# Storing a group's output: one transfer instead of four, in a fused attention and expert kernel on one core

## The chip, the core and the metric

The kernel runs on one core of one Trainium2 chip. The metric is the device time of a run in microseconds, lower is better. A profile is one execution of the program, recorded by the hardware; its times are microseconds from the start of the span, the time from the first to the last recorded instruction.

The engines go by the profile's names: PE (TensorE, matrix products), PEld (its weight loads), DVE (VectorE), ACT (ScalarE), POOL (GpSimd) and SP (SyncE, which only issues transfers). Transfers (DMA) are issued by SP, ACT and POOL and carried out by sixteen DMA engines.

## The reference

Four batches of 12480 tokens of 128 channels pass an attention with 32 inducing points, and then a two-layer net with a leaky activation:

```python
B, N, m, C = (4, 12480, 32, 128)
...
def mab(q, kv):
    s = scale * (q @ kv.transpose(0, 2, 1))
    s = s - s.max(-1, keepdims=True)
    a = np.exp(s)
    a /= a.sum(-1, keepdims=True) + 1e-09
    return a @ kv
h = mab(I, x)
return mab(x, h).astype(np.float32)
...
n_tokens, d_model, d_ff = (49920, 128, 2048)
...
h = x @ w_in
g = np.maximum(h, 0.0) + alpha * np.minimum(h, 0.0)
return (g @ w_out).astype(np.float32)
```

Inputs and output are float32. The output is 49920 x 128, 25.6 MB.

## The kernel before

A batch is cut into six blocks of 2048 tokens and a rest of 192; a block holds four groups of 512 tokens, so that a batch has 25 groups and the whole has 100. Phase A of a batch reads x (loads on POOL's queue, L412, L415, L427, with the change to bfloat16 on the way), transposes it (transfers on SP's queue, L432), takes scores against the inducing points (L553) and sums up the 32 vectors h of the batch. Batch 0's phase A stands by itself at the start; that of each later batch is woven into the groups of the batch before. Phase B works group by group. `b_scores` takes the scores of a block against h (ACT, L656), which go to DRAM (tile e2d, SP, L663); `b_rep` reads them back four times, once for each quarter of the partitions (tile rep, four transfers on SP, L671). `b_den` and `b_turn` do the same for the reciprocals of the softmax's sums (rt, L701; rdT, four transfers, L711).

`fill` makes the hidden layer: 16 small products of hW and rep for a group, each on a quarter of PE's rows (L383 is the line of the helper that records every product), with the positive part taken by ACT (L750) or DVE (L752) into a tile gt. `second` multiplies the gt tiles by W1 into the group's output bank, and after the last one calls `finish`.

`finish` is what the change touches. DVE transposes the bank in 32 x 32 blocks to the tile ot (L818; the pool has two buffers). POOL multiplies it by the reciprocals into the tile ob (L826; three buffers); for the group before the last, POOL does one half and DVE the other; for the last group DVE does all. Then the group is stored to DRAM (L851). Because of the block transpose, partition 32a + i of ob holds column block a (32 columns) of the tokens that belong to i, so the store writes rows of 32 floats, 128 bytes each: 512 rows for each of the four column blocks, 2048 for a group of 512 tokens, and 192 rows a block for the rest of a batch. The stores of most groups go out on POOL's queue; those of the last four groups on SP, ACT and POOL, by the table `queues`, where `to_end` counts the groups that are still to finish (0 is the last).

The order on each engine is fixed: `pin` ties every instruction to the one before it on its engine. What PE does in which order is written out in PLAN, one letter for each product; EVENTS and PAUSES say at which group and fill the loads, transposes, scores, reads and turns are issued. A store stands in POOL's order right behind the multiplication of its group, and the next x load, if there is one, behind the store. The batch changes are at groups 25, 50 and 75: the scores of the new batch's first block can be made only once its h is there (PAUSES, `hw1 bs10` at group 21, `hw2 bs20` at 46, `hw3 bs30` at 71), and its rep is read at the first fill of the new batch.

Of the kernel before, what the change touches and what calls it, by code (L numbers as in the profile page):

```python
# [19 lines left out]
NQ = 4  # L20
# [287 lines left out]
def kernel(  # L308
# [9 lines left out]
    nc = tc.nc  # L318
# [20 lines left out]
    def pin(bi):  # L339
        ins = bi.ins  # L340
        e = ins.engine
        if e in last:
            tc.add_manual_dep(
                ins,
                last[e],
                mybir.DependencyInfo(
                    mybir.DependencyClass.NoSync, mybir.DependencyReason.DATA
                ),
                reason="program order",
            )  # L350
        last[e] = ins.name
        return bi
# [361 lines left out]
    def shape_of(g):  # L714
        return (P, NB, 1) if g < NS * NQ else (PR, JR, 2)
# [68 lines left out]
    def second(i, n, r):  # L784
        st, g = group_of(i)
        pp, nb, _ = shape_of(g)
        t = pp * nb
        rows = slice(0, P) if r is None else slice(32 * r, 32 * r + 32)
        c, gt = live[i][n]
        first = i < LATE and n == 0 and not r  # L790
        if r and n == 0:
            hand_over(left[i])
        ins = mm(
            home[i][:, :t], W1[rows, c, :], gt[rows, :],
            start=first, stop=False, skip_group_check=True,
        )
        if n == KC - 1:
            if r == 3 or r is None:
                if i < LATE:
                    linear(st, g, home[i], 3, False)  # L800
                finish(st, g, home.pop(i))
                live.pop(i)
            else:
                left[i] = ins.ins
# [4 lines left out]
    def finish(st, g, acc):  # L809
        pp, nb, _ = shape_of(g)  # L810
        t = pp * nb
        s, q = divmod(g, NQ)
        rq = st.rden[s][:, :, :, q : q + 1]
        rbc = bass.AP(
            tensor=rq.tensor, offset=rq.offset, ap=[rq.ap[0], rq.ap[1], rq.ap[2], [0, 32]]
        )
        ot = ot_pool.tile([P, GRP], f32, name="ot", tag="ot")
        pin(nc.vector.transpose(out=ot[:, :t], in_=acc[:, :t]))  # L818
        ob = ob_pool.tile([P, GRP], f32, name="ob", tag="ob")
        to_end = B * NG - 1 - ended[0]  # L820
        ended[0] += 1

        def scaled(engine, k0, k1):
            w = t // nb
            part = rbc[:, k0:k1]
            pin(engine.tensor_tensor(  # L826
                out=ob[:, k0 * w : k1 * w].rearrange("p (k m c) -> p k m c", k=k1 - k0, c=32),
                in0=ot[:, k0 * w : k1 * w].rearrange("p (k m c) -> p k m c", k=k1 - k0, c=32),
                in1=part, op=MULT,
            ))  # L830

        if to_end == 0:
            scaled(nc.vector, 0, nb)
        elif to_end == 1:
            scaled(nc.gpsimd, 0, nb // 2)
            scaled(nc.vector, nb // 2, nb)
        else:
            scaled(nc.gpsimd, 0, nb)
        t0 = st.b * N + s * SUP
        if s < NS:  # L840
            dst = out[t0 : t0 + SUP, :].rearrange(
                "(i b q) (a k) -> q a i b k", b=t // 32, q=NQ, k=32)[q]
        else:
            dst = out[t0 : t0 + REM, :].rearrange("(i b) (a k) -> a i b k", b=t // 32, k=32)
        queues = {
            3: (nc.sync,) * 4, 2: (nc.scalar,) * 4,
            1: (nc.sync, nc.scalar, nc.gpsimd, nc.sync),
            0: (nc.scalar, nc.gpsimd, nc.scalar, nc.sync),
        }.get(to_end, (nc.gpsimd,) * 4)
        for a, queue in enumerate(queues):  # L850
            pin(queue.dma_start(  # L851
                out=dst[a],
                in_=ob[32 * a : 32 * a + 32, :t].rearrange("p (b k) -> p b k", k=32),
            ))
        st.rep.pop(g)

# [47 lines left out]
    for q in range(4):  # L904
        sl = slice(32 * q, 32 * q + 32)
        pin(nc.gpsimd.memset(pick[sl, q : q + 1], 1.0))
        for q2 in range(4):
            pin(nc.gpsimd.tensor_copy(
                out=fold[sl, 32 * q2 : 32 * q2 + 32], in_=ident32[sl, sl]
# [63 lines left out]
    n = len(parts)  # L973
# [81 lines left out]
    while pos < len(tokens):  # L1055
# [11 lines left out]
        elif tok in "wxyz":  # L1067
            r = "wxyz".index(tok)
            i, n = lane[r]
# [5 lines left out]
        elif tok == "v":  # L1075
            i, n = whole
# [47 lines left out]
```

## Time and profile before

| what | us |
|---|---|
| median of 3 runs | 541.08 |
| lowest, highest | 541.07, 543.59 |
| the profiled execution: span | 540.4 |
| PE busy | 526.3 |
| DVE busy | 504.2 |
| ACT busy | 496.3 |
| POOL busy | 394.7 |

The busy times are shares of one span; an engine that is busy is not thereby at its peak, since PE's products are pipelined and their ends are modelled. POOL's busy time holds its issues of transfers too. SP's and ACT's issues stand in the views as SPq and ACTq and are not counted as busy. In a group of instructions the columns are busy time, the mean time of one in ns, and the idle time of the engine just before them with what ended it. "To landing" of a transfer is the time from the start of its issue to the completion of its semaphore.

The transfers of the whole execution by queue (packets, MB, share of 16 engines' span), where q0 is POOL's, q1 SP's and q10 ACT's:

```profile
q0 software_dynamic: 19456, 38.62, 38.9%
q1 hardware_dynamic: 91984, 30.22, 32.9%
q8 instruction: 70, 1.15, 0.9%
q10 hardware_dynamic: 3200, 0.90, 0.7%
q14 instruction: 28, 0.23, 0.2%
```

### The profile page before, as it was taken

What the parts mean: (1) busy time and instruction counts of PE and PEld (TensorE: products, weight loads), DVE (VectorE), ACT (ScalarE), POOL (GpSimd) and SP (SyncE); (2) the same over time, 40 slices, a digit from 0 to 9 for tenths busy, and PEclk for the clock granted to TensorE, in tenths of its full rate; (3) what the DMA queues carried; (4) which work ended last, traced back from release to release, by engine and by line L of the source; (5) the groups of instructions that cost most, each with busy time, mean ns of one, the idle gap of its engine ahead of it and who ended that gap; (6) DMA issues with size and microseconds to landing.
All of it is one profiled execution on the core that took longest, in us unless ns stands there. A gap on an engine that the chain in (4) does not pass through costs nothing.

```text
span 540.4 us, 21603 instructions
## 1 busy us (share of the span) xinstructions
PE 526.3 (97%) x8988; PEld 332.7 (62%) x8988; DVE 504.2 (93%) x865; ACT 496.3 (92%) x994; POOL 394.7 (73%) x574
## 2 busy tenths in 40 slices
PE   4999999999999999999999999999999999999996
PEld 4655566566567566666667666666666566666653
DVE  3699999999989999999998999999999999999994
ACT  2499999999989999999999999999999999999950
POOL 5553778687667987687687987776767876776764
PEclk9999999999999999999999999999999999999998
DMA  8999999987799898887799797864354344334324
GB/s 197 212 186 139 182 185 156 170 142 113 112 175 149 134 160 152 162 129 145 117 153 166 117 164 158 168 101 113 66 93 113 66 96 112 70 89 108 68 42 85
DMA packets 114738, 71.12 MB, mean 132 GB/s; under 512 B 86784, under 2 KB 102784, under 8 KB 114640
## 3 DMA queue, kind: packets, MB, share of 16 engines
q0 software_dynamic: 19456, 38.62, 38.9%
q1 hardware_dynamic: 91984, 30.22, 32.9%
q8 instruction: 70, 1.15, 0.9%
q10 hardware_dynamic: 3200, 0.90, 0.7%
q14 instruction: 28, 0.23, 0.2%
HBM read 41.00 MB, written 28.95 MB: 129 GB/s over the span
## 4 chain that ended last, share of the span: by engine, by line
PE 90%; DMA 4%; DVE 2%; ACT 1%; POOL 1%; issue 1%; SPq 0%; POOLq 0%; DVEq 0%
PE bank L383 90%; DMA xn<-in_x_dram 2%; DMA rep<-e2d 1%; ACT gt L750 1%; DVE gt L752 1%; DMA e2d<-e 1%; POOL xn L412 0%; DVE ot L818 0%; PE bank L458 0%; ACT e L656 0%; DVE xT L461 0%; POOL ob L826 0%; DVE fr L608 0%; SPq L671 0%; POOL out_dram L851 0%
## 5 line engine op out<-in xcount | busy, mean ns | idle before, releaser
L383 PE MATMUL bank<-gt,W 32*128 32x512 bf16 (+1 forms) x6256 | 480.3, 371 | 0.1
L750 ACT ACTIVATE gt<-bank 128x512 bf16<-128x512 f32 (+1 forms) x906 | 464.5, 612 | 6.9 <-PE bank L383 4.6
L752 DVE TENSOR_SCALAR gt<-bank 128x512 bf16<-128x512 f32 (+1 forms) x662 | 417.7, 677 | 9.9 <-PE bank L383 6.1
L383 PE MATMUL bank<-rep,hW 32*128 32x512 bf16 (+1 forms) x1600 | 418.4, 368 | 1.5 <-DMA rep<-e2d 1.3
L383 PEld LDWEIGHTS <-W 32*128 32x128 bf16 x6256 | 264.4, 92 | 146.5 <-issue 46.6
L851 POOL DMA_DIRECT2D out_dram<-ob x386 | 247.3, 669 | 37.7 <-POOL ob L826 30.4
L826 POOL TENSOR_TENSOR ob<-ot,rdT 128x512 f32<-128x512 f32 (+2 forms) x99 | 106.3, 1074 | 93.8 <-DVE ot L818 79.5
L383 PEld LDWEIGHTS <-hW 32*128 32x128 bf16 x1600 | 136.9, 92 | 20.8 <-issue 5.1
L818 DVE STREAM_TRANSPOSE ot<-bank 128x512 f32<-128x512 f32 (+1 forms) x100 | 69.9, 699 | 6.7 <-PE bank L383 5.6
L383 PE MATMUL bank<-rep,hA 32*128 32x512 bf16 (+1 forms) x100 | 36.1, 367 | 0.0
L427 POOL DMA_DIRECT2D xn<-in_x_dram x32 | 20.7, 663 | 0.1
L481 ACT ACTIVATE e1t<-bank 128x256 bf16<-128x256 f32 (+2 forms) x14 | 5.0, 356 | 10.8 <-PE bank L383 10.8
L461 DVE COPY xT<-bank 128x1024 bf16<-128x1024 bf16 (+1 forms) x13 | 8.5, 650 | 4.9 <-PE bank L458 4.4
L383 PE MATMUL bank<-xT 32*128 32x512 bf16 x81 | 12.5, 376 | 0.0
L553 ACT ACTIVATE e<-bank 128x512 bf16<-128x512 f32 x18 | 11.0, 610 | 0.2 <-PE bank L383 0.2
L656 ACT ACTIVATE e<-bank 128x512 bf16<-128x512 f32 x18 | 11.1, 614 | 0.1
L383 PEld LDWEIGHTS <-xT 128*128 128x128 bf16 (+1 forms) x177 | 8.0, 97 | 4.1 <-issue 1.5
L383 PEld LDWEIGHTS <-hT 128*32 128x32 bf16 (+1 forms) x122 | 3.6, 93 | 11.0 <-issue 10.9
L383 PE MATMUL bank<-xT,hT 128*32 128x512 bf16 (+1 forms) x98 | 10.3, 388 | 0.0
L383 PEld LDWEIGHTS <-hA 32*128 32x128 bf16 x100 | 9.2, 92 | 1.8 <-issue 0.6
L458 PE MATMUL bank<-ident,xn 128*128 128x128 bf16 x96 | 9.0, 249 | 1.0 <-DVE xn L963 0.9
L412 POOL DMA_DIRECT2D xn<-in_x_dram x11 | 6.2, 583 | 3.3 <-DMA xn<-in_x_dram 2.5
(87 smaller groups left out, 131.7 us busy)
## 6 DMA issues: line engine op xcount, KB each, us to landing
out_dram<-ob POOLq DMA_DIRECT2D x373, 64.0 KB, 3.2
rep<-e2d SPq DMA_DIRECT2D x92, 128.0 KB, 3.2
xn<-in_x_dram POOLq DMA_DIRECT2D x37, 256.0 KB, 5.5
e2d<-e SPq DMA_DIRECT2D x24, 128.0 KB, 3.6
xn<-in_x_dram POOLq DMA_DIRECT2D x4, 512.0 KB, 8.2
rdT<-rt SPq DMA_DIRECT2D x96, 8.0 KB, 2.6
early<-in_moe_w_out_dram POOLq DMA_DIRECT2D x4, 256.0 KB, 10.6
xT<-xn SPq DMA_TRANSPOSE x36, 5.2
```

Source lines behind the costliest of these rows:

```text
L383: return pin(nc.tensor.matmul(o, lhsT, rhs, start=start, stop=stop, **kw))
L412: pin(nc.gpsimd.dma_start(out=xn[:, q0:q1, :], in_=src[:, q0:q1, :]))
L427: pin(nc.gpsimd.dma_start(out=st.xn[u][:, part, :], in_=src[:, part, :]))
L458: pin(nc.tensor.transpose(tp[:, k * P : (k + 1) * P], xn[:, q, j * C : (j + 1) * C], ident[:]))
L461: pin(nc.vector.tensor_copy(out=st.xT[:, u, qs[0] : qs[-1] + 1, :].rearrange("c q t -> c (q t)"), in_=tp[:, : len(qs) * GRP],))
L553: pin(nc.scalar.activation(out=e1[:], in_=ps[:], func=EXP, scale=scale, accum_out=st.es[:, u : u + 1]))
L656: pin(nc.scalar.activation(out=e2[:].rearrange("p (t j i) -> p t j i", j=n, i=32), in_=turned(ps[:pp, :w], n), func=EXP, scale=scale_of(st ...
L750: pin(nc.scalar.activation(out=gt[:, :w], in_=ps[:, :w], func=RELU))
L752: pin(nc.vector.tensor_relu(gt[:, :w], ps[:, :w]))
L818: pin(nc.vector.transpose(out=ot[:, :t], in_=acc[:, :t]))
L826: pin(engine.tensor_tensor(out=ob[:, k0 * w : k1 * w].rearrange("p (k m c) -> p k m c", k=k1 - k0, c=32), in0=ot[:, k0 * w : k1 * w].rearr ...
L851: pin(queue.dma_start(out=dst[a], in_=ob[32 * a : 32 * a + 32, :t].rearrange("p (b k) -> p b k", k=32),))
```

## The change

In `finish`, the four transfers of a group, one for each column block, become one whose DRAM side has the block as its outermost dimension. For a group of 512 tokens the DRAM side was 512 rows of 32 floats from 32 partitions; it is now 4 x 512 x 32 from 128 partitions. The queues of the last four groups were SP four times (`to_end` 3), ACT four times (2), SP, ACT, POOL, SP (1) and ACT, POOL, ACT, SP (0). They are now POOL (3), SP (2), POOL (1), and for the last group two transfers of two column blocks each, on ACT and on SP (0; 2 x 192 x 32 from 64 partitions). All other groups stay on POOL. On POOL the store of `to_end` 3 stands between two multiplications (L826) that followed each other before. Nothing else moves in the order of any engine.

```diff
         queues = {
-            3: (nc.sync,) * 4, 2: (nc.scalar,) * 4,
-            1: (nc.sync, nc.scalar, nc.gpsimd, nc.sync),
-            0: (nc.scalar, nc.gpsimd, nc.scalar, nc.sync),
-        }.get(to_end, (nc.gpsimd,) * 4)
-        for a, queue in enumerate(queues):
+            2: (nc.sync,), 1: (nc.gpsimd,), 0: (nc.scalar, nc.sync),
+        }.get(to_end, (nc.gpsimd,))
+        n = NQ // len(queues)
+        for k, queue in enumerate(queues):
             pin(queue.dma_start(
-                out=dst[a],
-                in_=ob[32 * a : 32 * a + 32, :t].rearrange("p (b k) -> p b k", k=32),
+                out=dst[n * k : n * k + n],
+                in_=ob[32 * n * k : 32 * n * (k + 1), :t].rearrange("p (b k) -> p b k", k=32),
             ))
```

## The prediction

> **What bounds the kernel now.** I read the busy shares first, then a table of stages, then the list of waits, and last the chain of waits at the places where TensorE is not full.
>
> ```profile
> span 540.4 us, 21603 instructions
> PE 526.3 (97%) x8988; PEld 332.7 (62%) x8988; DVE 504.2 (93%) x865; ACT 496.3 (92%) x994; POOL 394.7 (73%) x574
> ...
> 0.00:50.00 50.00, 42.15 (x686) 26.88 (x686) 35.28 (x69) 32.03 (x64) 24.67 (x57) 1.00 0.97 186
> 50.00:130.00 80.00, 79.97 (x1395) 49.17 (x1391) 77.39 (x132) 79.61 (x165) 60.81 (x87) 1.00 0.95 159
> 130.00:160.00 30.00, 28.45 (x505) 17.45 (x499) 27.88 (x53) 27.24 (x57) 21.45 (x31) 1.00 0.94 141
> 160.00:270.00 110.00, 110.00 (x1961) 72.10 (x1954) 108.13 (x185) 109.03 (x219) 86.85 (x123) 1.00 0.85 144
> 270.00:340.00 70.00, 70.00 (x1282) 46.45 (x1281) 66.36 (x111) 69.60 (x141) 58.40 (x83) 1.00 0.88 150
> 340.00:400.00 60.00, 60.00 (x1048) 37.87 (x1043) 58.48 (x103) 59.04 (x118) 43.26 (x61) 1.00 0.57 108
> 400.00:505.00 105.00, 105.00 (x1825) 65.88 (x1818) 103.62 (x172) 104.62 (x206) 79.00 (x110) 1.00 0.40 92
> ```
>
> The columns of the table are the stretch, its length, the busy time of PE, PEld, DVE, ACT and POOL, the granted clock, the DMA engines' busy share and GB/s. From 50 to 505 us PE is idle for 0.03 + 1.55 us, DVE and ACT are nearly as full, and the clock is at full speed. GpSimd has a quarter of its time free. The second thing to see is the DMA column: until 340 us the sixteen DMA engines are 85 to 97% busy, so a transfer there stands in a crowd.
>
> ```profile
> PE bank L383 <- DMA rep<-e2d: 1.3, 1, 1.3
> ...
> 141.13 4.54 DMA e2d<-e
> ...
> 146.56 5.67 DMA rep<-e2d
> ...
> 152.28 7.93 PE bank L383 x130
> ```
>
> The one wait of the body is a DMA's. At the change from batch 0 to batch 1 the scores go out to DRAM (e2d, L663) and come back four times (rep, L671), and PE has nothing in hand: it waits 1.3 us. The same pair stands at the next two batch changes, with a margin:
>
> ```profile
> L671 SPq DMA_DIRECT2D rep<-e2d x4: 303/424/429, 269.8 to 271.1; - x4
> ...
> DMA to landing us min/median/max: 4.2/4.4/4.6
> ...
> 277.05 0.37 PE L383 MATMUL bank<-rep,hW 32*128 32x512 bf16 x2
> ...
> L671 SPq DMA_DIRECT2D rep<-e2d x4: 302/426/433, 396.6 to 397.9; - x4
> ...
> DMA to landing us min/median/max: 4.6/4.6/4.6
> ...
> 404.17 0.37 PE L383 MATMUL bank<-rep,hW 32*128 32x512 bf16 x1
> ```
>
> The last of four lands at 271.1 + 4.6 = 275.7 and is read at 277.05 (margin 1.4 us); at the third change at 397.9 + 4.6 = 402.5, read at 404.17 (margin 1.7 us). So three places have margins of 0, 1.4 and 1.7 us against a later landing.
>
> **The change, part by part.** *GpSimd's issues.*
>
> ```profile
> L851 POOL DMA_DIRECT2D out_dram<-ob x386 | 247.3, 669 | 37.7 <-POOL ob L826 30.4 <-issue 6.7 <-DVE ob L826 0.4
> L826 POOL TENSOR_TENSOR ob<-ot,rdT 128x512 f32<-128x512 f32 x95 | 103.6, 1090 | 90.9 <-DVE ot L818 76.6 <-DMA rdT<-rt 13.8
> L427 POOL DMA_DIRECT2D xn<-in_x_dram x32 | 20.7, 663 | 0.1
> ```
>
> Per group four issues of 669 ns become one. Its price is bounded by 663 ns (the x load: 128 rows, though a store of 512 rows costs no more) and 4 x 669 = 2.7 us (as if each row cost). I take the near end, 0.7 us: a fourfold count of rows made no difference. So GpSimd gets back about 2.0 us in each of 98 groups, some 195 us, and none of it is on the path: GpSimd waited for DVE's ot for 76.6 us already, and would wait longer.
>
> *How wide a store runs.* This is the step that decides. For four stores by GpSimd in a quiet stretch, and then for four by SyncE, the transfer view gives:
>
> ```profile
> DMA packets 128, 0.26 MB, mean 67 GB/s; under 512 B 64, under 2 KB 64, under 8 KB 128
> ...
> q0 software_dynamic: 128, 0.26, 33.3%
> ...
> q1 hardware_dynamic: 2112, 0.26, 38.6%
> ```
>
> A GpSimd store is 16 data packets and 16 tiny ones; a SyncE store is 528 packets, 512 rows of 128 B and 16 tiny ones. I read the 16 as one closing write for each of 16 engines. In work, the first window (3.9 us) gives 0.333 x 16 x 3.9 = 20.8 us of engine time for a group, the second (4.0 us) 0.386 x 16 x 4.0 = 24.7 us, or 11.7 ns a packet. Over 16 engines that is 1.3 and 1.5 us.
>
> In all present transfers the outermost counts, on both sides, divide by 16 (32 partitions against 512 or 192 rows of DRAM in a store; 16, 32, 96 or 128 partitions elsewhere). In the new store the DRAM side is led by the four column blocks (4 x 512 x 32), in the last group by two (2 x 192 x 32). If a transfer is dealt to engines by its outermost count, the new ones run on 4 and 2 engines, with the same work in all. The trace has no such shape, so both ends stand: 16 engines (1.3 and 1.5 us a group) or four (20.8 / 4 = 5.2 us by GpSimd, 24.7 / 4 = 6.2 us by SyncE or ScalarE). I take four, and two in the last group: all that the 16 closings have shown is shapes that could be cut in 16.
>
> [...]
>
> *The body.* With 5.2 us of store on four engines in every group of 5.1 us (25 groups stand between the reads at 277.05 and 404.17), some four engines always carry a burst, and an e2d or rep transfer that needs all 16 ends with the slowest. Each of the pair waits between 0 and a whole burst, 5.2 us; half is 2.6, and 1.3 us of a spread store stand in its way already, so 1.3 more for each, 2.6 for the pair. Less the margins: 2.6 + 1.2 + 0.9 = 4.7 us for the three batch changes. The ends are 0 and 3 x 10.4 - 3.1 = 28 us. What stands behind: PE's order is fixed, so a late rep stops all fills, DVE and ACT run dry behind it, and on SyncE the transposes and rdT loads queued after rep move by as much.
>
> *The end.* Four groups finish in the last 11 us. The last but three goes from SyncE to GpSimd's queue, the next from ScalarE to SyncE, the next from three queues to GpSimd, the last from three to ScalarE and SyncE.
>
> ```profile
> 528.40 1.17 POOL L826 TENSOR_TENSOR ob<-ot,rdT 128x512 f32<-128x512 f32 x1
> 530.06 1.07 POOL L826 TENSOR_TENSOR ob<-ot,rdT 128x512 f32<-128x512 f32 x1 [0.48 <-DVE ot L818]
> ...
> 533.22 0.72 DVE L818 STREAM_TRANSPOSE ot<-bank 128x512 f32<-128x512 f32 x1
> ...
> 535.85 0.65 POOL L851 DMA_DIRECT2D out_dram<-ob  x1 [0.96 <-POOL ob L826]
> ...
> 536.28 0.36 DVE L826 TENSOR_TENSOR ob<-ot,rdT 128x192 f32<-128x192 f32 x1
> 536.67 1.49 ACTq L851 DMA_DIRECT2D out_dram<-ob  x2
> ...
> out_dram<-ob SPq DMA_DIRECT2D x6, 64.0 KB, 2.2
> out_dram<-ob POOLq DMA_DIRECT2D x5, 64.0 KB, 2.2
> out_dram<-ob ACTq DMA_DIRECT2D x5, 64.0 KB, 2.4
> out_dram<-ob ACTq DMA_DIRECT2D x2, 24.0 KB, 2.2
> ```
>
> A store lands 2.2 us after its issue; 1.5 / 4 = 0.4 us of that is movement, so about 1.2 us stand before it and 0.6 behind. Today the last issue starts at 536.67 + 0.62 = 537.3 and lands at 539.5, and the span ends 0.9 us later. Now with narrow stores:
> (a) GpSimd's new issue comes at about 529.9, ahead of its next multiplication. That one moves from 530.06 to 530.6 and ends at 531.7; DVE's next transpose into ot comes only at 533.22, so nobody waits. The store lands at 529.9 + 1.2 + 5.2 + 0.6 = 536.9.
> (b) SyncE's store, issued at 531.7, moves from 532.9 to 539.1.
> (c) GpSimd's store of the last but one group is issued at 535.85, one issue where three queues shared four, and lands at 535.85 + 1.2 + 5.2 + 0.6 = 542.9. It alone would end the span at 543.8, 3.4 us later.
> (d) The last group's ob is the third buffer back, which store (a) reads. So DVE's multiplication waits from 536.28 to 536.9, a wait that is hidden now, and the two stores are issued at 537.3. Each is 384 rows, 384 x 11.7 ns / 2 = 2.25 us on two engines. On the same two, and these among SyncE's four, they start at 538.5, find 0.6 us of (b) left, take 4.5, and land at 538.5 + 0.6 + 4.5 + 0.6 = 544.2: the span ends at 545.1, 4.7 us later. On engines apart they land at 541.4 and (c) ends the span.
> So the end costs 3.4 to 4.7 us; I take 4.7, since a deal that starts at a fixed engine puts SyncE's and ScalarE's on the same ones.
>
> Sum: 540.4 + 4.7 + 4.7 = 549.8 us of span. The median of the runs shown (541.08) is 0.7 above the span, so 550.5, say **550.5 us**.
>
> **The rivals.** *Only SyncE's and ScalarE's stores are narrow.* GpSimd's packets are of 4 KB, each of 32 rows, another way of cutting, and it may still deal 128 partitions over all engines. Then the body stands, (c) lands at 539.0, and the last pair, issued at 536.7, finds 1.2 us of (b) left: 537.9 + 1.2 + 4.5 + 0.6 = 544.2, the same end, 4.7 us later: 540.4 + 4.7 + 0.7 = 545.8 (542.5 if the pair runs apart). [...] *All stores stay wide.* For it: every transfer in the trace is. Then the body is unchanged, the last group loses its second ScalarE issue (0.6 us), and (c) lands at 535.85 + 2.2 + 0.9 = 539.0 or, if its issue costs 2.7 us, at 541: 540.4 - 0.5 + 0.7 = 540.6, up to 542. *Faster:* the time that GpSimd gets back lets its x loads out up to 2 us sooner and thins the crowd of the first 340 us, so that e2d and rep land sooner at 152 us. Its place is that wait and its price is at most PE's idle time there, 1.55 us, and 0.5 at the end: 541.1 - 2.1 = 539.0. For more, PE itself would have to run faster, and the windows after 160 us leave it no gap. It decides if stores are wide and that wait goes.
>
> **How the numbers follow.** No change is what lies within 0.5%, 538.4 to 543.8. Narrow stores on all queues: 0.48, 550.5 (its own range 544.5 to 567: 3.4 us at the end and none in the body, up to 4.7 at the end and 21 of the body's 28). Narrow on SyncE and ScalarE alone: 0.22, 545.8, a quarter of it with the pair apart. Wide: 0.20, 540.6. The faster rival: 0.05; its 539.0 lies within 0.5%, but I count 0.04 beyond, as no row bounds what a thinner crowd would do before 130 us. Something else, mostly a longer backlog in the crowded first 340 us: 0.05. The range is 540.5 to 567: it leaves out the faster rival, half of the wide one and the longest backlogs. Slower 0.70, within 0.5% 0.26, faster 0.04.
>
> **What would show it.** In the transfer view SyncE's whole group would have 4 tiny packets and the last pair 2 each, where every transfer now has 16; SyncE's store would land after some 8 us and GpSimd's after 7. PE would wait for rep at about 152, 277 and 404 us, and DVE's last multiplication for GpSimd's store (a). GpSimd's busy time would fall from 394.7 to some 215 us (98 issues of 0.7 for 386). I am wrong if GpSimd's store lands in less than 4.5 us (the body stands), if SyncE's does (wide), or if GpSimd's one issue takes near 2.7 us.

## The result, and the profile after

The changed kernel takes 1510.22 us (median of 4 runs, 1503.11 to 1513.39) against 541.08 us: 2.79 times as long, with a 95% interval of 2.78 to 2.80. The profiled execution has a span of 1506.0 us, 965.6 us more than the 540.4 of before. Here and below, runs more than 1.5% above the fastest of their kernel are left out of comparisons.

The busy shares, the clock and the transfers by queue of the kernel after:

```profile
span 1506.0 us, 21313 instructions
PE 728.5 (48%) x8987; PEld 428.3 (28%) x8988; DVE 526.9 (35%) x865; ACT 529.2 (35%) x994; POOL 453.7 (30%) x286
...
PEclk9976767766677666777668677777767767776755
...
q0 software_dynamic: 33280, 41.40, 42.7%
...
L850 POOL DMA_DIRECT2D out_dram<-ob x98 | 304.0, 3102 | 1012.6 <-issue 940.7
...
out_dram<-ob POOLq DMA_DIRECT2D x95, 256.0 KB, 14.8
```

No engine is full any more: PE fell from 97% to 48% of the span, POOL from 73% to 30%. DVE and ACT do the same work in nearly the same time (526.9 and 529.2 us, against 504.2 and 496.3); PE's busy time grew, 526.3 to 728.5 us, with a granted clock of mostly six to seven tenths (0.719 in the mean, where it was 0.996). POOL's busy time rose, 394.7 to 453.7 us, though it issues 98 stores instead of 386: one issue (L850) costs 3.10 us instead of 0.67. And q0, POOL's queue, carries 33280 packets where it had 19456. So the question is what everybody waits for. The list of waits says it (us in total, times, longest):

```profile
POOL out_dram L850 <- issue: 940.7, 87, 14.7
...
DVE ot L818 <- POOL ob L826: 781.2, 92, 15.5
...
PE bank L383 <- DVE ot L818: 692.3, 87, 13.6
...
PE bank L383 <- DMA rep<-e2d: 2.4, 1, 2.4
```

Read from the bottom of the chain: PE waits for DVE to empty a group's bank, DVE for GpSimd to free ot, and GpSimd stands in front of its store (L850, L851 before) for 940.7 us in 87 waits. "issue" means that the engine waited for nothing that the profile shows. What it waited for shows when the landing time of the stores is laid beside their issues. The timeline of POOL over two groups, and the view of the tile out_dram in the same stretch:

```profile
1025.95 1.51 POOL L826 TENSOR_TENSOR ob<-ot,rdT 128x512 f32<-128x512 f32 x1
1040.13 3.14 POOL L850 DMA_DIRECT2D out_dram<-ob  x1 [12.67 <-issue]
1042.86 1.51 POOL L826 TENSOR_TENSOR ob<-ot,rdT 128x512 f32<-128x512 f32 x1
1055.07 3.13 POOL L850 DMA_DIRECT2D out_dram<-ob  x1 [10.70 <-issue]
```

```profile
DMA to landing us min/median/max: 14.6/14.8/15.0
```

The store issued at 1040.13 lands 14.6 us later, at 1054.76, and the next one starts at 1055.07, 0.31 us after that. This holds nearly all along: in the records of the trace 82 of 97 stores start 0.31 to 0.34 us after the one before has landed. From this store to the next it is 14.94 us: 3.14 of issue, 1.10 of what is left of the multiplication, 10.70 of waiting. GpSimd's first store is issued at 49.6 us and its last at 1490.5, 14.85 us a store in the mean. Against the 5.1 us of a group before, 98 x (14.85 - 5.1) = 956 us, nearly the whole loss of 965.6.

What the store does in these 15 us shows in the transfers by queue between 1040.1 and 1055.0, which hold one store by GpSimd:

```profile
q0 software_dynamic: 272, 0.29, 39.0%
```

64 data packets of 4 KB and 16 of 4 bytes, the closings, are 80 of the 272. The other 192 have 128 bytes each in the records. The bytes written to HBM are the same before and after (28.95 MB), so nothing more arrives in DRAM:

```profile
HBM read 41.00 MB, written 28.95 MB: 129 GB/s over the span
...
HBM read 41.00 MB, written 28.95 MB: 46 GB/s over the span
```

The records name no engine, nor what the small packets are for, but packets can be counted: 64 is 4 x 16 and 192 is 12 x 16, and between 400 and 1400 us at most four of the 4 KB packets are under way at once in 98% of the time in which any is, and at most twelve of the small ones. In engine time the store takes 0.39 x 16 x 14.9 = 93 us instead of 20.8: by the records of one store 33.0 us in the 64 data packets, which take longer each, and 59.8 in the small ones.

Two predicted marks are there too. In the records SyncE's joined group has 4 closings and the last two stores 2 each (4 bytes each). And the last stores in the timeline of the end:

```profile
1478.24 13.03 SPq L850 DMA_DIRECT2D out_dram<-ob  x2
...
1490.34 0.36 DVE L826 TENSOR_TENSOR ob<-ot,rdT 128x192 f32<-128x192 f32 x1 [11.71 <-DMA out_dram<-ob]
1490.47 3.13 POOL L850 DMA_DIRECT2D out_dram<-ob  x1 [11.68 <-issue]
```

DVE's last multiplication waits for GpSimd's store of three groups before, for 11.71 us, and GpSimd's last store, 14.2 us from issue to landing at 1504.66, ends the span.

### The profile page after: what moved, and what is told of

It is laid out like the page before. It is cut to its first block, busy times and chain, and to the rows that moved or that the text cites. A ratio compares the mean times of both kernels' runs of the same rounds, so it can differ in the third digit from the quotient of the medians.

```text
span 1506.0 us, 21313 instructions
## 1 busy us (share of the span) xinstructions
PE 728.5 (48%) x8987; PEld 428.3 (28%) x8988; DVE 526.9 (35%) x865; ACT 529.2 (35%) x994; POOL 453.7 (30%) x286
## 3 DMA queue, kind: packets, MB, share of 16 engines
q0 software_dynamic: 33280, 41.40, 42.7%
HBM read 41.00 MB, written 28.95 MB: 46 GB/s over the span
## 4 chain that ended last, share of the span: by engine, by line
issue 70%; POOL 21%; DMA 4%; PE 2%; SPq 1%; DVE 1%; POOLq 0%; ACT 0%; DVEq 0%
POOL out_dram L850 11%; POOL ob L826 8%; PE bank L383 2%; POOL xn L427 2%; DMA out_dram<-ob 1%; DMA xn<-in_x_dram 1%; SPq L671 1%; DMA rep<-e2d 1%; DMA rt<-rd 0%; DVE gt L752 0%; DMA rdT<-rt 0%; DMA e2d<-e 0%; POOLq L1118 0%; POOLq L826 0%; POOL xnr L415 0%
## 5 line engine op out<-in xcount | busy, mean ns | idle before, releaser
L383 PE MATMUL bank<-rep,hW 32*128 32x512 bf16 (+1 forms) x1600 | 549.5, 477 | 576.4 <-DVE ot L818 573.9
L750 ACT ACTIVATE gt<-bank 128x512 bf16<-128x512 f32 (+1 forms) x906 | 494.2, 602 | 772.0 <-PE bank L383 767.9
L383 PE MATMUL bank<-gt,W 32*128 32x512 bf16 (+1 forms) x6255 | 671.9, 472 | 20.3 <-DVE gt L752 19.9
L850 POOL DMA_DIRECT2D out_dram<-ob x98 | 304.0, 3102 | 1012.6 <-issue 940.7
L383 PEld LDWEIGHTS <-W 32*128 32x128 bf16 x6256 | 360.5, 111 | 773.3 <-issue 664.0
L752 DVE TENSOR_SCALAR gt<-bank 128x512 bf16<-128x512 f32 (+1 forms) x662 | 435.6, 680 | 139.6 <-PE bank L383 132.9
L383 PEld LDWEIGHTS <-hW 32*128 32x128 bf16 x1600 | 160.2, 110 | 86.6 <-issue 67.9
L826 POOL TENSOR_TENSOR ob<-ot,rdT 128x512 f32<-128x512 f32 (+2 forms) x99 | 146.1, 1480 | 16.1 <-DMA rdT<-rt 14.1
L383 PE MATMUL bank<-rep,hA 32*128 32x512 bf16 (+1 forms) x100 | 50.7, 513 | 0.0
L383 PE MATMUL bank<-xT,IT 128*32 128x512 bf16 x72 | 10.1, 527 | 21.1 <-DVE ot L818 21.1
L383 PEld LDWEIGHTS <-hA 32*128 32x128 bf16 x100 | 11.9, 119 | 2.2 <-issue 1.2
## 6 DMA issues: line engine op xcount, KB each, us to landing
out_dram<-ob POOLq DMA_DIRECT2D x95, 256.0 KB, 14.8
```

The lines of the kernel that those rows point to most:

```text
L383: return pin(nc.tensor.matmul(o, lhsT, rhs, start=start, stop=stop, **kw))
L750: pin(nc.scalar.activation(out=gt[:, :w], in_=ps[:, :w], func=RELU))
L752: pin(nc.vector.tensor_relu(gt[:, :w], ps[:, :w]))
L826: pin(engine.tensor_tensor(out=ob[:, k0 * w : k1 * w].rearrange("p (k m c) -> p k m c", k=k1 - k0, c=32), in0=ot[:, k0 * w : k1 * w].rearr ...
L850: pin(queue.dma_start(out=dst[n * k : n * k + n], in_=ob[32 * n * k : 32 * n * (k + 1), :t].rearrange("p (b k) -> p b k", k=32),))
```

## The experiments

The expectations weigh a few readings. One is that the leading count of the store's DRAM side decides (four, if the transfer is dealt to engines by it); another is that the number of rows in one transfer decides (2048 where it was 512), whatever leads. For the later runs the distance of the rows in DRAM was added. Each kernel's time stands beside a median of 541.58 or 541.74 us for the kernel before on the same chip. A time without an interval is of a single run.

**GpSimd's stores in four again, the end as changed.** Against the changed kernel:

```diff
-            2: (nc.sync,), 1: (nc.gpsimd,), 0: (nc.scalar, nc.sync),
-        }.get(to_end, (nc.gpsimd,))
+            2: (nc.sync,), 0: (nc.scalar, nc.sync),
+        }.get(to_end, (nc.gpsimd,) * 4)
```

> GpSimd's stores are four again in every group that it stores, each led by 512 (or 192) rows of DRAM; SyncE's group of four blocks and the last pair of two blocks stay joined. Theory A (GpSimd's joined store, led by 4, is dealt badly: data on four engines, work without data on the other twelve, and the next store cannot be issued before it has landed): the body is as before, and only the end pays for the narrow stores of SyncE and ScalarE, 0 to 4.7 us: 541 to 546 us. Theory B (a store of 2048 rows is slow whatever queue and shape it has): SyncE's one such store takes about 15 us too, and since it is issued some 9 us before the end, the time is 546 to 552. SyncE's store should show 4 tiny packets, the last two 2 each.

Measured: 551.89 us, ratio 1.018 (1.015 to 1.021). The body is that of before (PE is busy for 110.00 us of the 110 from 160 and for 105.00 of the 105 from 400 us here too), so all but 10 us of the loss come from GpSimd's joined stores, and these 10 us from the end. The time alone lies in the range of theory B and not in that of A, so it doesn't decide between them; the packets of the end and the next kernel do. The end of this kernel, timeline and transfers of the last 17 us (the row DMA is the busy share of the engines in 40 slices):

```profile
533.40 8.47 SPq L850 DMA_DIRECT2D out_dram<-ob  x2
...
534.96 1.13 ACTq L850 DMA_DIRECT2D out_dram<-ob  x1
```

```profile
DMA  2000212927848644333311111212212211100000
...
q1 hardware_dynamic: 2438, 0.31, 14.2%
...
q10 hardware_dynamic: 386, 0.05, 2.7%
```

q1's 2438 packets are 2048 rows and 4 closings of SyncE's group and 384 rows and 2 closings of its half of the last; q10's 386 are 384 and 2. Before, each store had 16 closings. The second half of the busy row stands at one and two tenths of sixteen engines until 548 us. The records don't name the engine; that ScalarE's and SyncE's last stores share two engines, and that these are also two of SyncE's four, is my estimate from the times. ScalarE's 384 packets take 7.1 us (539.50 to 546.58), where 384 / 2 packets of 15 ns, one behind the other, would be 2.9. If the busier of a shared pair runs 512 + 192 + 192 = 896 packets from 534.73 to 548.22, that is 15.1 ns a packet.

**One store of a group with one level of 2048 rows.** Against the kernel before; most groups go to another place of the output (rows in the order of partitions), so that the DRAM side has one level of 2048 rows of 128 bytes (written as 128 x 16 rows at one stride):

```diff
         }.get(to_end, (nc.gpsimd,) * 4)
+        if s < NS and to_end > 3:
+            queues = (nc.gpsimd,)
+            dst = out[t0 : t0 + SUP, 32 * q : 32 * q + 32].rearrange("(p b) k -> p b k", b=t // 32)[None]
+        n = NQ // len(queues)
         for a, queue in enumerate(queues):
...
-                in_=ob[32 * a : 32 * a + 32, :t].rearrange("p (b k) -> p b k", k=32),
+                in_=ob[32 * n * a : 32 * n * (a + 1), :t].rearrange("p (b k) -> p b k", k=32),
```

> One GpSimd store of 2048 rows for each full group but the last four, as in the changed kernel, but the DRAM side is led by 2048 rows at one stride; the rows of a block go to other places of the output (it is permuted within a block). The rest of a batch and the last four groups are stored as before. Theory A (the leading count of 4 is the cause): about 541 us, the store lands in 3.4 to 5 us, 64 data packets of 4096 B and none of 128 B. Theory B (the number of rows in one transfer is the cause): about 1500 us and a landing near 15 us.

Measured: 542.42 us, ratio 1.001 (0.999 to 1.003), no change. Its page:

```profile
span 541.1 us, 21338 instructions
...
PE 524.9 (97%) x8987; PEld 330.9 (61%) x8988; DVE 504.0 (93%) x865; ACT 496.7 (92%) x994; POOL 259.9 (48%) x295
...
q0 software_dynamic: 14992, 38.60, 36.8%
...
out_dram<-ob POOLq DMA_DIRECT2D x93, 256.0 KB, 4.5
```

The same 2048 rows in one transfer land in 4.5 us instead of 14.8. So joining as such costs nothing, and the number of rows isn't the cause. (It is a probe and no replacement, since the rows go to other places.) Nor does it bring anything: GpSimd's busy time falls by 135 us (394.7 to 259.9) and the time stays, because GpSimd was hardly on the path (1% of the chain that ended last, before and here).

**Two stores of two blocks a group.** Against the kernel before, with the changed kernel's loop:

```diff
-        }.get(to_end, (nc.gpsimd,) * 4)
+        }.get(to_end, (nc.gpsimd,) * 2)
```

> GpSimd stores a group by two transfers of two column blocks, led by 2 on the DRAM side, in every group but the last four, which are stored as before. Theory A: data on two engines, 512 rows on each, just as many on each engine as in the changed kernel, so that each of the two stores takes as long as its one store: 25 to 30 us a group, 2400 to 2900 us. Theory B: 1024 rows cost half of 2048, so a group costs the same 15 us (about 1500 us) or less.

Measured: 2744.21 us. Page and timeline:

```profile
q0 software_dynamic: 58432, 44.01, 39.2%
...
out_dram<-ob POOLq DMA_DIRECT2D x186, 128.0 KB, 14.1
```

```profile
1503.71 3.11 POOL L852 DMA_DIRECT2D out_dram<-ob  x1 [9.76 <-issue]
1517.58 3.10 POOL L852 DMA_DIRECT2D out_dram<-ob  x1 [10.76 <-issue]
```

Half the bytes, led by two, land no sooner (14.1 us), and the next waits again: 13.87 us between issues, twice in a group. A store of 2 x 512 rows is as long as one of 4 x 512 (14.1 and 14.8 us). The records show 224 packets of 128 bytes a store, 14 x 16.

**Four stores a group, each led by four.** Against the kernel before; most groups go to other places of the output. Each store takes 512 rows as before, but of all partitions, and its DRAM side is led by the four column blocks:

```diff
+        whole_rows = s < NS and to_end > 3
+        src = ob[:, :t].rearrange("p (b k) -> p b k", k=32)
+        m = t // 32 // NQ
         for a, queue in enumerate(queues):
+            if whole_rows:
+                part = out[t0 + GRP * a : t0 + GRP * (a + 1), :].rearrange(
+                    "(i b q) (a k) -> q a i b k", b=m, q=NQ, k=32)[q]
...
+                out=part if whole_rows else dst[a],
+                in_=src[:, m * a : m * a + m, :] if whole_rows else src[32 * a : 32 * a + 32],
```

> GpSimd stores a full group by four transfers of 512 rows and 64 KB, as before the change, but each has all four column blocks and a quarter of the rows, so that it is led by 4 (4 x 128 x 32); the tokens of a block are permuted in the output. The last four groups are stored as before. Theory A: the leading count decides, and the time is far above 541: 900 to 1500 us, less than the changed kernel's 1510 only as far as several small stores can be under way at once. Theory B: as before the change, 541 us.

Measured: 941.46 us. Page and timeline:

```profile
DMA  9999999999989999999999999999987677777666
```

```profile
499.35 6.17 POOL L857 DMA_DIRECT2D out_dram<-ob  x4 [0.46 <-POOL ob L826]
...
507.60 1.07 POOL L826 TENSOR_TENSOR ob<-ot,rdT 128x512 f32<-128x512 f32 x1 [2.09 <-DVE ot L818]
```

Four narrow stores follow each other here without waiting, in 6.17 us, though each takes 10.9 us to land. The DMA row stands at eight tenths and more for three quarters of the span; in the last quarter it is lower, and GpSimd itself is full, with 6.1 us of issues and most of the rest in its multiplication, at 7.6 us a group. The wait is there too, but rarer: 49.2 us in 20 waits for "issue", most of which end 0.31 to 0.34 us after a landing, with six of the small stores under way. So leading by four costs some 400 us with 512 rows a store as well: a group takes 9.4 us in the mean instead of 5.1. The rest, from there to 15 us (1510 us in all), I put down to the wait for one large store at a time; that share is argued and not measured by itself.

**One store of a group led by 16, and by 8.** Against the kernel before, the same edit as for one level of 2048 rows, with again another place in the output:

```diff
+            dst = out[t0 : t0 + SUP, 32 * q : 32 * q + 32].rearrange("(r o) k -> o r k", o=16)[None]
```

and the same with o=8.

> One GpSimd store of 2048 rows for each full group but the last four, with a DRAM side of two levels as in the changed kernel, but led by 16 (16 x 128 x 32); the rows of a block go to other places of the output. The rest of a batch and the last four groups are stored as before. Theory A (the leading count decides how many engines carry data): 16 engines, no packets without data, about 541 us. Theory C (a DRAM side of two levels is what GpSimd's queue handles badly, whatever its leading count): about 1500 us, with packets of 128 B in GpSimd's queue.

> The same with a DRAM side of 8 x 256 x 32. Theory A: eight engines carry 8 data packets of 4096 B each, the other eight run 8 packets of 128 B each, so a store adds 64 packets of 128 B to GpSimd's queue; half as many rows on an engine as in the changed kernel, so a landing of 6 to 8 us. If the next store still had to wait for the landing, a group would cost 7 to 9 us and the whole 700 to 900; if two such stores fit, the engines' work (64 x 0.58 + 64 x 0.31 = 57 us, 3.6 us on each of 16) allows 541 to 600. Theory C: about 1500.

Measured: 555.34 us led by 16, ratio 1.027 (1.020 to 1.033), and 669.69 us led by 8. By 16 and then by 8, from the two pages:

```profile
q0 software_dynamic: 14992, 38.60, 37.4%
...
out_dram<-ob POOLq DMA_DIRECT2D x93, 256.0 KB, 5.2
```

```profile
q0 software_dynamic: 20944, 39.36, 50.9%
...
out_dram<-ob POOLq DMA_DIRECT2D x93, 256.0 KB, 9.2
```

Led by 16 there is no packet more than with 2048 rows; led by 8 there are 5952 more, which is 93 x 64, or 8 x 8 packets in each store. Only the leading count differs, so it is what makes the small packets. It also sets how many data packets are under way at once: in the records from 400 us on, the 4 KB packets under way at once are at most 16 with one level of 2048 rows or led by 16, 8 led by 8, 4 led by 4 and 2 led by 2, in 95% or more of the time in which any is. The fewer they are, the longer each takes: 0.28 us with 2048 rows, 0.30 led by 16, 0.37 by 8, 0.53 by 4.

With 8 the stores don't wait for each other's landing (landing 9.2 us, while three can be issued 3.3 us apart). The time lies between the two that were expected, and the landing above 6 to 8 us. PE waits for transposes of x (47.9 us) and for rep (29.4 us) that come late, with q0 at 50.9% where it was 36.8% with one level of 2048 rows. The run led by 16 is a miss: the reading by the leading count had it at the time of before, and it is some 14 us above. PE waits there for three late transposes of x (the waits, then the chain of waits); these are 7.0 of the 12.2 us that its span is longer than that with one level, and the rest lies in PE's busy time, 530.1 us against 524.9, at a mean granted clock of 0.988 against 0.997:

```profile
PE bank L383 <- DMA xT<-xn: 7.0, 3, 2.7
```

```profile
210.55 10.07 DMA xT<-xn
...
278.99 9.63 DMA xT<-xn
...
346.89 9.74 DMA xT<-xn
```

**Is it the distance of the rows?** Led by 16 or by 4, the rows that follow each other under one leading index were first 16 or 4 rows of the output apart. The next two kernels place them one behind the other, within the places of two blocks (against the kernel before; other places of the output again; o=16 and o=4):

```diff
+            p0 = st.b * N + s // 2 * 2 * SUP
+            dst = out[p0 : p0 + 2 * SUP, 32 * q : 32 * q + 32].rearrange(
+                "(o h r) k -> h o r k", o=16, h=2)[s % 2][None]
```

> As the store led by 16 (553 to 555 us), but the rows of one engine's share stand 512 B apart in DRAM, as in the wide store of 542 us, where they stood 8 KB apart; the blocks of a batch are interleaved in pairs in the output. The rest of a batch and the last four groups are stored as before. If the distance of the rows is what cost those 12 us, 541 to 543 us. If it is the DRAM side of two levels itself, 553 to 556.

> The same with a DRAM side of 4 x 512 x 32 and rows 512 B apart, so that the leading count is the changed kernel's and the addresses are the wide store's. Theory A (the leading count): about 1500 us, a landing near 14 us and 192 packets of 128 B a store. If the addresses of the changed kernel (rows 2 KB apart, four column blocks of the same 512 B) were what made its store slow, 541 to 700.

Measured: 549.99 and 552.98 us led by 16 (two more: 560.16 and 561.62), and 1480.27 us led by 4. Both kernels are near their counterparts (551.90 to 559.31, and 1510.22), so the addresses decide neither; led by 16 they may account for a few us. Led by 4, from the page and the waits:

```profile
q0 software_dynamic: 32848, 40.89, 42.7%
...
out_dram<-ob POOLq DMA_DIRECT2D x93, 256.0 KB, 14.8
```

```profile
POOL out_dram L857 <- issue: 900.7, 84, 14.7
```

32848 - 14992 = 17856 = 93 x 192 small packets, as in the changed kernel, and the same wait. What is left for the 8 to 14 us led by 16 is that its DRAM side has two levels (16 x 128 rows) where the other has one of 2048; why that is slower stays open.

**SyncE issues all stores, in one and in four.** Against the kernel before; the first with the changed kernel's loop:

```diff
-        }.get(to_end, (nc.gpsimd,) * 4)
+        }.get(to_end, (nc.sync,) * 1)
```

and (nc.sync,) * 4 in the second.

> All stores but the last four groups' go out on SyncE's queue, joined to one and led by 4. No packets without data are expected there (SyncE's joined store has 4 closings). Theory A: 2048 rows on the same four engines each time, 512 x 12 to 15 ns = 6.1 to 7.7 us a group against 5.1 us of compute, so these four engines bound the kernel: 650 to 850 us, far below the 1510 of GpSimd's queue, and no wait for the landing before the next issue. If the narrowness alone, without the packets that carry no data, were what costs 15 us a group, 1500.

> The same on SyncE's queue with four stores a group, led by 512 (or 192). All theories: 541 to 580 us, what the queue's order costs; it is the reference for the kernel with one store on SyncE.

Measured: 908.7 us in one, 643.51 us in four. Both are above what was expected (850 and 580 at most). On SyncE's queue the stores stand in order with the transposes and reads, and that alone costs 102 us. Joining costs 265 us on top. SyncE's joined store has no small packets beyond its closings (q1 carries 285136 packets against 290896 with four stores, 60 fewer closings in each of 96 groups). An estimate: if it takes the same four engines each time, 2048 packets of 16.3 ns in the mean (packets' records) over four are 8.35 us, more than a group's 5.1; which engines it takes is not shown. The two waits that tell it, of the kernel with one store:

```profile
POOL ob L826 <- DMA out_dram<-ob: 281.3, 46, 13.5
...
PE bank L383 <- DMA rep<-e2d: 183.6, 26, 14.0
```

## Why the prediction was wrong

The direction and its root were right: a store led by four runs narrower, with at most four of its data packets under way at once (98% of the time), where a store with one level of 2048 rows has up to 16. The size was wrong by two orders: the sum had 9.4 us of loss, and there are 965.6. Two steps failed: that a narrow store has "the same work in all", and that none of GpSimd's time "is on the path".

- **How wide a store runs** ("with the same work in all"). This is the first step that failed. That a store is dealt to engines by its outermost count no row of before showed, and no run names an engine; what the runs showed are the 4 and 2 closings of SyncE's and ScalarE's joined stores, with no packet beside these and their rows, and GpSimd's data packets, at most k at once in a store led by k (95% or more of the time). GpSimd's store led by four has, beside its 64 data packets, 192 small ones. The term of 20.8 us of engine time measured 91 to 93. The 5.2 us of movement is 10.0 in one store (1447.62 to 1457.65, issue at 1443.86, landed at 1458.44): its data packets take 33.0 us of engine time, which would be 8.2 for each of four engines. The 1.2 us before the first packet are 3.8; the issue alone takes 3.1. So the landing of about 7 us became 14.8. The trace of before couldn't show this: all its leading counts divide by 16, and the store led by 16 has no such packets.
- **None of it on the path.** This is the second step, and the one that sets the time. The prediction had GpSimd with spare time in each group and counted bursts of 5.2 us only as delays to other transfers; nothing in the sum made one store wait for the one before. But GpSimd's next store starts when the last has landed (940.7 us in 87 waits), so its 15 us became the period of the kernel. With the predicted landing of 7.0 us and this wait, a group would have taken 7.3 us and the kernel some 98 x (7.3 - 5.1) = 216 us more (an estimate). The place to ask was the 5.2 us against a group's 5.1: a store as long as a group leaves no room for an error in its size. Of the stated rivals none had GpSimd's queue as the bound.
- **GpSimd's issues** (0.7 us for one). One takes 3.10 us, above even the upper bound of 2.7. The stated mark, an issue near 2.7 us, came, but not for its reason, that each row costs: the same 2048 rows cost 1.13 us led by 2048, 1.10 led by 16 and 1.80 led by 8, so in these runs the issue goes with the leading count. GpSimd's busy time, which was to fall to some 215 us, rose to 453.7. That its issue time is worth nothing while it is off the path was right: 135 us less of it left the time at 542.42.
- **The body** (4.7 us, at most 28). Its mechanism, late reads at the three batch changes, is nearly absent: PE waits for rep once, for 2.4 us. At 15 us a group everything else is early. Where narrow stores don't wait for each other it is there: led by 8, PE waits 29.4 us for rep.
- **The end** (4.7 us). The 4.7 stood on a deal that starts at a fixed engine, which no run shows, since the records don't name the engines; the times with GpSimd's stores in four fit one pair of engines for the last two stores (7.1 us for ScalarE's 384 packets, where two engines of their own were estimated at 2.9). SyncE's group landed 11.9 us after its issue (533.40 to 545.3 in the records), where 8 were expected. The end's size, with GpSimd's stores in four, is 550.0 - 540.4 = 9.6 us. Packets took 15.1 ns and not 11.7, which on 896 is 3.0 us; SyncE's store was issued at 533.4 and not 531.7, since GpSimd's four issues of the group before held up its next multiplication, 1.7 us. 4.7 + 3.0 + 1.7 = 9.4. In the changed kernel itself GpSimd's own last store ends the span.
- **The rivals.** That only SyncE's and ScalarE's stores are narrow falls with GpSimd's data packets, at most four at once; that all stay wide falls with these and with the 4 and 2 closings. The faster rival's gain, GpSimd's time for the x loads, didn't come when it was given back without the narrow stores (542.42).

Shown by the runs: the leading count of the DRAM side decides how many data packets are under way at once and how many small packets there are, and with them the time (555, 670 and 1510 us for one store led by 16, 8 and 4); the number of rows doesn't (542.42 us with 2048 in one level), nor do the addresses (1480.27 us led by four with near rows); a large narrow store by GpSimd is waited for until it lands (82 of 97 start 0.31 to 0.34 us after). Not shown: what the small packets are for, which engines run them, and why the wait exists. Full stores with 512 rows to a leading index were never under way together (the changed kernel, and the two of two blocks), three with 256 rows were (led by 8), and in the kernel with four stores up to seven with 128 were. None of the versions tried beats the kernel before; the one that joins without a cost is equal to it.

## What to carry to other kernels

Before joining stores, look at what stands outermost on DRAM's side: joining four stores put a 4 there (1510.22 us), while a join with 2048 rows outermost, to other places of the output, was free (542.42 us against 541.74). When a cost estimate for one transfer comes out as long as the loop that issues it, the issuing queue is the next bound to check, whatever spare time its engine has: here 5.2 us stood against a group's 5.1, and the landing measured 14.8. And work that is given back to an engine off the path is worth nothing until something on the path needs it: here 135 us of GpSimd's time bought none.

## What the hardware did that was not expected

- A store by GpSimd led by k has packets of 128 bytes beside its data: 64 of them at k = 8, 192 at k = 4, 224 at k = 2 (half as many bytes), none at k = 16. The times are 669.69, 1510.22, 2744.21 (two stores a group) and 555.34 us. The data packets under way at once are at most k (95% or more of the time), and each takes longer at a small k: 0.30 us at 16, 0.53 at 4.
- GpSimd's next store starts 0.31 to 0.34 us after a large narrow one has landed (82 of 97), with nothing in the profile that it waits for but "issue".
- The issue of one store of 2048 rows by GpSimd costs from 1.10 (led by 16) to 3.10 us (led by 4).
- Two short stores on two queues, 384 rows each, behind a store of 2048 rows (GpSimd's stores in four): ScalarE's 384 packets took 7.1 us, and from the first packet of the three to the last it was 13.5 us (534.73 to 548.22), with the sixteen engines one to two tenths busy in the last 6.
- Stores of 16 x 128 rows cost 14 us of the kernel's time (8 and 11 in the two runs with near rows) where those of 2048 rows at one stride cost none, with the same packets, the same bytes and a landing 0.7 us longer (5.2 against 4.5).
